# Token lists in tiles of their own, two gathers in flight, and accumulating stores that do not wait for each other, in a fused attention and top-2 mixture-of-experts kernel

## The chip, the cores and the metric

The kernel runs on one core of a Trainium2 chip. The core has five engines that each take their own instructions strictly in order: TensorE (PE), VectorE (DVE), ScalarE (ACT), GpSimd (POOL) and SyncE (SP, which here only issues transfers); 16 DMA engines serve all transfers. The metric is the device time of one execution in microseconds (us): for the kernel before, the median of three runs.

## The reference

Attention over 32 learned memory slots, then a noisy top-2 gate over 8 experts, then the two chosen experts for each of 4608 tokens:

```python
a = softmax(phi, axis=2)                                  # 8 batches x 8 heads x 576 x 32
k_m = einsum('bhsm,bhsd->bhmd', a, k); v_m = einsum('bhsm,bhsd->bhmd', a, v)
x = softmax(q @ k_m.T / 8) @ v_m                          # reshaped to [4608, 512]
z = x @ w_gate + log1p(exp(x @ w_noise)) * noise          # [4608, 8]
top2, top2_w = the two largest of z, and softmax over these two
for e in range(8):
    for k in range(2):
        mask = top2[:, k] == e
        h = relu(x[mask] @ w1[e])                         # 512 -> 1024
        out[mask] += top2_w[mask, k] * (h @ w2[e])        # 1024 -> 512
```

The answer must be close to float32. So every large product is made of float16 halves: a value is split into a high and a low part, and three products (high by high, high by low, low by high) are summed.

## The kernel before, in words

**Attention and routing (to about 277 us).** The tokens are worked on in four pairs of batches of nine 128-token tiles each. The pieces of work of attention, of the routing and of the first expert's early groups are sorted by a table of times written by hand (`PRI`), and a scheduler, which simulates the engines, sets from these priorities the order in which each engine gets its instructions. `gate()` decides for a pair of batches which two experts each token goes to and which slot of that expert's list it takes. It writes one (token row, weight) entry per token and choice into the table `lst` in device memory: a scatter on POOL (L514), one for each tile and each of the two choices, 72 in all. The last pair is gated in two parts, of five tiles (10 scatters) and of four (8 scatters).

**The lists.** Each expert has a list of 1216 slots: nine tiles of 128 tokens and a tail of 64. `lists(e, t0, t1)` reads a piece of it into the tile `lt` (SP, L609). Tiles of that name come from a pool with two buffers: the list of expert e+1 takes the buffer of expert e-1. Each read names all scatters recorded so far as things to wait for; a scatter that comes after a read of `lst` waits for that read.

**Groups.** Experts work on groups of four, four and two list tiles (4 x 128, 4 x 128, 128 + 64 tokens). Expert 0 has four groups, and its first three, of two tiles, start before the routing is complete; so does the fetching for expert 1's first group, whose four tiles surely hold only tokens of earlier pairs. For each tile of a group:

- `gather()` fetches the tile's token rows by an indirect DMA on POOL (`gtile`, L652, 80 in all), splits them into float16 halves on ACT (`ghalf`, L665) and DVE (L666), and puts the transposed halves into `xt` by a transposing DMA on SP (L667). `gtile` and `ghalf` have two buffers each, `xt` three.
- `mm1()` makes the hidden layer in eight blocks of 128 features: 12 matmuls into a PSUM tile `mp` (L702, three buffers), a relu on ACT (`r`, L706) and the split on DVE (`hh`, L707; `hl`, L708).
- `mm2()` makes the output of each 128-token tile from 24 matmuls (L734; `ps`, three buffers); ACT scales it by the token weights (`y`, L738, two buffers). The tail of 64 goes through L744, L748, L749 and L750.
- `put()` adds `y` to the rows of `out` that the list names: an accumulating indirect DMA on POOL (L759, 74 from `y` and 6 early ones from `stg`). All of them write the same tensor, so each waits until the one before has landed.

**The order in the experts' phase.** The loop over (expert, group) starts the gathers two groups ahead of the matmuls and steps through them between pieces of `mm1` and `mm2`. At the first group of expert e it also issues the loads of expert e+1's weights (`stg`, L550, SP: two matrices of four 512 KB pieces), and reads expert e+1's list. The weights are split on ACT (`wh`, L584) and DVE (`wl`, L585) after a maximum over each piece (`wam`, L567). SP's queue thus holds list reads, weight loads and transposes in one row, POOL's queue gathers and stores. What of these stands first in a queue holds up all that stands behind it until its own wait ends. The last tile of expert e-1 is stored after the matmuls of that expert's last group, and the list of expert e+1, for which it frees the buffer, is read behind it.

Of the kernel before, what the change touches and what calls it, by code (L numbers as in the profile page):

```python
# [20 lines left out]
NP = B // 2  # L21
# [18 lines left out]
F32G = 0  # L40
HC = 2.0 ** -14
# [4 lines left out]
def tile_attn_moe(ctx, tc, q_t, phi_t, kv, wgn, noise, w1, w2, out, dbg=None):  # L46
# [56 lines left out]
    # row h*32+m of a group keeps its own head's columns  # L103
# [14 lines left out]
    def late_consts():  # L118
        scr = ld.tile([128, 2, S], F32, name="qs", bufs=BUF["qs"])
        scr = scr.rearrange("p a s -> p (a s)")  # L120
        pidx = scr[:, 0:128].bitcast(I32)
        G.iota(pidx, pattern=[[1, 128]], base=0, channel_multiplier=-1)
        V.tensor_scalar(tri, pidx, 0.0, None, op0=OP.is_gt)
        G.iota(iota_e, pattern=[[0, NJ], [1, E]], base=0, channel_multiplier=0,
               allow_small_or_imprecise_dtypes=True)
        G.iota(eoff, pattern=[[0, NJ], [LCAP, E]], base=0, channel_multiplier=0,
               allow_small_or_imprecise_dtypes=True)
        V.memset(base, 0.0)
        G.memset(zt, 0.0)
        # token lists start as trash rows with weight zero  # L130
        pl = scr[:, 424:424 + 2 * NPRE].rearrange("p (c t) -> p c t", t=2)
        pi = scr[:, 128:128 + NPRE].bitcast(I32)
        G.iota(pi, pattern=[[1, NPRE]], base=0, channel_multiplier=NPRE)
        V.tensor_scalar(pi, pi, TRASH - 1, None, op0=OP.bitwise_and)
        G.memset(pl, 0.0)
        V.tensor_copy(pl[:, :, 0].bitcast(I32), pi)
        nc.sync.dma_start(lst.rearrange("(p c) t -> p (c t)", p=128), pl.rearrange("p c t -> p (c t)"))
        nc.sync.dma_start(xs[0:TRASH, :].rearrange("(a p) d -> p a d", p=128), zt[:, None, :].to_broadcast([128, TRASH // 128, DM]))
# [12 lines left out]
    def overflow_count():  # L151
        # 128-token blocks of each expert beyond its static slots, and the sums of their counts
# [26 lines left out]
    def overflow():  # L179
        # tokens of an expert beyond its static slots, 128 at a time  # L180
# [116 lines left out]
    def a_s(u):  # L297
        """Scores, memory slots on the partitions; a batch's 64 tokens beside the next one's in tile 4."""
        b, g = divmod(u, 2)
        if g == 0:  # L300
            ST[b] = wk.tile([128, 2, 640 - b % 2 * 128], F32, name="st%d" % (b % 2), bufs=BUF["st%d" % (b % 2)])
        for o, n in ((0, 512), (512, 64)) if b % 2 == 0 else ((0, 64), (64, 512)):
            sp = px.tile([128, 512], F32, name="xp")
            for hp in range(2):
                T.matmul(sp[hp * 64:(hp + 1) * 64, 0:n], KB[u][:, hp * 64:(hp + 1) * 64],
                         QS[u][:, hp, o:o + n], start=True, stop=True)
            dst = ST[b][:, g, o:o + n] if b % 2 == 0 else ST[b][:, g, 0:512] if o else ST[b - 1][:, g, 576:640]
            A.activation(dst, sp[:, 0:n], AF.Copy)
# [11 lines left out]
    def scale_chain(pool, psp, am, n, tag):  # L320
        # a power of two that brings the largest magnitude below 2^10
# [102 lines left out]
    scatters, gated = [], set()  # L424

    def gate(P, j0, j1):
# [15 lines left out]
        # log1p(exp(z)) = ln(1+u) u / ((1+u)-1), and u where 1+u == 1  # L442
# [32 lines left out]
        # slot of a token in its experts' lists: earlier pairs, earlier tiles, earlier rows  # L475
# [36 lines left out]
        for j in range(nj):  # L512
            for k in range(2):
# [3 lines left out]
                for o in scatters:  # L517
                    tc.declare_no_dep(sc.ins, o.ins, reason="distinct list slots")
                scatters.append(sc)
# [5 lines left out]
    late = {}  # L525
    W, WS, WU, LT, XT, HT = {}, {}, {}, {}, {}, {}

    def rows(t):
        return 128 if t < NTL else TAIL
# [7 lines left out]
    def w_load(e, i):  # L537
        if e == 0 and F32G:
            # expert 0's early groups multiply in float32, while the other engines are busy
# [18 lines left out]
    def w_prep(e, i):  # L558
        """Split one of the expert's matrices, scaled by a power of two, into high and low parts."""
# [42 lines left out]
    def lists(e, t0, t1):  # L602
        if e not in LT:
            LT[e] = msm.tile([128, NTL + 1, 2], F32, name="lt")
# [3 lines left out]
        def read(dst, src):  # L608
            d = nc.sync.dma_start(dst, src)  # L609
            for s in scatters:  # L610
                tc.add_manual_dep(d.ins, s.ins.name, SYNC, reason="list entries")
# [25 lines left out]
    def gather(e, g):  # L637
# [10 lines left out]
        XT[e, g] = xt  # L648
        for i, t in enumerate(ts):
            n = rows(t)  # L650
            gt = mpool.tile([128, DM], F32, name="gtile", bufs=2)
            G.indirect_dma_start(  # L652
                out=gt[:n], out_offset=None, in_=xs[0:seen, :],
                in_offset=bass.IndirectOffsetOnAxis(ap=LT[e][:n, t, 0:1].bitcast(I32), axis=0))
            yield
            if e == 0 and g < F32G:
                ps = mps.tile([128, 512], F32, name="mp")
                for c in range(4):
                    T.transpose(ps[:, c * 128:c * 128 + n], gt[:n, c * 128:(c + 1) * 128], identf[:n, :n])
                A.activation(xt[:, :, i * 128:i * 128 + n],  # L660
                             ps.rearrange("p (c n) -> p c n", c=4)[:, :, 0:n], AF.Copy)
                yield
                continue
            gh = mpool.tile([128, 2, DM], F16, name="ghalf", bufs=2)
            A.activation(gh[:n, 0], gt[:n], AF.Copy)  # L665
            V.tensor_tensor(gh[:n, 1], gt[:n], gh[:n, 0], OP.subtract)  # L666
# [3 lines left out]
    def hbuf(e, g):  # L670
        if e == 0 and g < 3:
            # the eight row blocks of the hidden layer, float32
# [81 lines left out]
    def put(e, t, y):  # L754
# [7 lines left out]
        if e == E - 1:  # L762
            # of two neighbouring tiles, unused slots have trash rows of their own
            if (t, NTL) == (NTL - 1, late.get("last")):
                tc.declare_no_dep(d.ins, late["lastd"].ins, reason="distinct rows")
            late["last"], late["lastd"] = t, d
# [24 lines left out]
    def unit(u):  # L791
        # the first units have no work beside them: their stages follow one another at once
# [38 lines left out]
    def early(e, g, t, t1, md):  # L831
        """Work of expert e's token group g before the routing is complete."""
# [80 lines left out]
    if dbg is not None:  # L913
        nc.sync.dma_start(dbg["xs"], xs[TRASH:, :])
        nc.sync.dma_start(dbg["lst"], lst)
        nc.sync.dma_start(dbg["cnt"], base)
# [10 lines left out]
    wt(1, 4, NTL + 1)  # L927
    seq = [(0, 3), (1, 1), (1, 2)] + [(e, g) for e in range(2, E) for g in range(3)]
# [4 lines left out]
    for k, (e, g) in enumerate(seq):  # L933
        if e and g == (1 if e == 1 else 0):
            if e + 1 < E:
# [3 lines left out]
                lists(e + 1, 0, NTL + 1)  # L939
# [59 lines left out]
```

## Time and profile before

| | |
|---|---|
| time, three runs | 1083.1, 1087.76, 1075.59 us (median 1083.1) |
| the profiled execution | 1082.0 us, its span 1082.0 us |
| PE busy | 965.0 us (89%), 5632 matmuls |
| DVE, ACT, POOL busy | 530.8, 371.5, 331.0 us |
| DMA | 147.93 MB, mean 137 GB/s |
| attention and routing, with early groups of expert 0 | to about 277 us |
| experts | 277 to 1067 us, then the last stores |
| PE idle in the experts' phase, 297 to 1067 us | 39.3 us, in a dozen gaps of up to 9.47 us |

PE is busy for most of the experts' phase, so the gaps between its matmuls are what to look at there: for each the trace names what ended it. "Releaser" means the instruction or transfer that the waiting one waited for last. The granted clock (PEclk) tells where PE ran below full speed; its mean in a window of 1.00 is full speed, and 0.50 would be half throughout.

### The profile page before, as it was taken

The numbers are of one execution on the slowest core, as the hardware profiler recorded it, in microseconds if no ns is written. First come the engines' busy times: TensorE is split into PE (matmuls) and PEld (weight loads), VectorE is DVE, ScalarE is ACT, GpSimd is POOL, SyncE is SP. The second block draws the span as 40 slices with busy tenths as digits, with TensorE's granted clock in tenths as the row PEclk, the third lists the DMA queues.
The fourth block names the chain that finished last, engine by engine and source line by source line (L and its number), as shares of the span: only waits on it lengthen the run. The fifth ranks groups of instructions, "written<-read, shape, count | busy, mean of one in ns | idle before, by whom it ended". The sixth has DMA issues, their size and how long they took to land.

```text
span 1082.0 us, 15210 instructions
## 1 busy us (share of the span) xinstructions
PE 965.0 (89%) x5632; PEld 496.2 (46%) x5632; DVE 530.8 (49%) x1391; ACT 371.5 (34%) x760; POOL 331.0 (31%) x314
## 2 busy tenths in 40 slices
PE   5897888486986978998998999999899999999995
PEld 3464555254433434543553454446344544454453
DVE  3689787574242523874273338744523573323212
ACT  4676562332122312532232234333222543221211
POOL 2133637654432123223213131322231143211111
PEclk9899889689998989999999999999999999999998
DMA  9999999767374365665445256645453436430212
GB/s 313 336 364 353 226 340 270 166 131 114 69 171 74 98 93 112 142 164 133 84 117 118 39 91 187 178 88 77 124 115 67 87 78 125 74 54 8 37 24 31
DMA packets 144874, 147.93 MB, mean 137 GB/s; under 512 B 94176, under 2 KB 103456, under 8 KB 144800
## 3 DMA queue, kind: packets, MB, share of 16 engines
q1 hardware_dynamic: 125344, 107.02, 36.5%
q0 software_dynamic: 19456, 39.93, 21.6%
q8 instruction: 45, 0.74, 0.3%
q14 instruction: 29, 0.24, 0.1%
HBM read 86.77 MB, written 40.22 MB: 117 GB/s over the span
## 4 chain that ended last, share of the span: by engine, by line
PE 46%; DMA 15%; DVE 6%; issue 3%; POOL 1%; ACT 1%; POOLq 0%; ACTq 0%; SPq 0%; DVEq 0%
PE ps L734 25%; PE mp L702 20%; DMA gtile<-xs,lt 7%; DMA out<-y,lt 5%; DVE wl L585 3%; DMA xt<-ghalf 2%; DMA stg<-in_w 1%; DVE wam L567 1%; PE ps L744 1%; DMA lt<-lst 1%; POOL gtile L652 1%; POOL out L759 1%; DVE hh L707 0%; ACT ghalf L665 0%; DVE hl L708 0%
## 5 line engine op out<-in xcount | busy, mean ns | idle before, releaser
L702 PE MATMUL mp<-xt,wh 128*128 128x512 f16 (+2 forms) x1408 | 283.8, 339 | 22.5 <-ACT r L706 13.0
L759 POOL DMA_INDIRECT out<-y,lt x74 | 117.5, 1588 | 367.8 <-ACT y L738 164.2
L702 PEld LDWEIGHTS <-wh 128*128 128x128 f16 x1600 | 152.2, 99 | 154.9 <-issue 40.1
L734 PE MATMUL ps<-wh,hh 128*128 128x512 f16 x496 | 186.6, 384 | 12.1 <-DVE hh L707 6.1
L707 DVE CAST hh<-r 128x512 f16<-128x512 f32 (+3 forms) x200 | 72.6, 365 | 241.7 <-ACT r L706 240.9
L734 PE MATMUL ps<-wh,hl 128*128 128x512 f16 x496 | 189.8, 384 | 0.7 <-DVE hl L708 0.6
L734 PE MATMUL ps<-wl,hh 128*128 128x512 f16 x496 | 189.3, 383 | 0.0
L734 PEld LDWEIGHTS <-hh 128*128 128x128 f16 x1152 | 114.0, 99 | 144.8 <-issue 10.8
L706 ACT ACTIVATE r<-mp 128x512 f32<-128x512 f32 (+3 forms) x200 | 96.9, 492 | 228.9 <-PE mp L702 161.8
L652 POOL DMA_INDIRECT gtile<-xs,lt x80 | 89.5, 1118 | 228.8 <-DVE ghalf L666 154.0
L702 PE MATMUL mp<-xt,wl 128*128 128x512 f16 (+2 forms) x704 | 153.0, 340 | 0.0
L666 DVE TENSOR_TENSOR ghalf<-gtile,ghalf 128x512 f16<-128x512 f32 x80 | 55.1, 690 | 155.6 <-ACT ghalf L665 155.6
L708 DVE TENSOR_TENSOR hl<-r,hh 128x512 f16<-128x512 f32 (+3 forms) x200 | 113.4, 570 | 4.8
L665 ACT ACTIVATE ghalf<-gtile 128x512 f16<-128x512 f32 x80 | 50.2, 628 | 188.9 <-DMA gtile<-xs,lt 138.0
L702 PEld LDWEIGHTS <-wl 128*128 128x128 f16 x800 | 76.8, 99 | 59.6 <-issue 3.3
L567 DVE TENSOR_REDUCE wam<-stg 128x1 f32<-128x512 f32 x128 | 81.7, 678 | 34.2 <-DMA stg<-in_w 34.1
L734 PEld LDWEIGHTS <-hl 128*128 128x128 f16 x576 | 57.2, 99 | 86.7 <-issue 18.3
L738 ACT ACTIVATE y<-ps,wlu 128x512 f32<-128x512 f32 x62 | 42.1, 683 | 154.6 <-PE ps L734 121.6
L514 POOL DMA_INDIRECT lst<-gent,gidx x72 | 72.3, 1004 | 23.5 <-issue 19.0
L585 DVE SCALAR_TENSOR_TENSOR wl<-stg,wsc,wh 128x512 f16<-128x512 f32 x96 | 65.3, 742 | 0.0
L584 ACT ACTIVATE wh<-stg,wsc 128x512 f16<-128x512 f32 x96 | 60.1, 709 | 4.2 <-DVE wsc L332 4.1
L414 PE MATMUL xp<-vb,at 128*128 128x272 f32 (+1 forms) x160 | 48.1, 443 | 14.3 <-ACT xr L416 14.3
(167 smaller groups left out, 819.0 us busy)
## 6 DMA issues: line engine op xcount, KB each, us to landing
stg<-in_w SPq DMA_DIRECT2D x64, 512.0 KB, 7.0
kvs<-in_kv SPq DMA_DIRECT2D x16, 1024.0 KB, 10.3
out<-zt SPq DMA_DIRECT2D x38, 256.0 KB, 5.1
qs<-in_q_t SPq DMA_DIRECT2D x16, 576.0 KB, 10.0
xs<-xr SPq DMA_DIRECT2D x36, 256.0 KB, 6.4
phs<-in_phi_t SPq DMA_DIRECT2D x16, 288.0 KB, 8.7
kvs<-in_kv SPq DMA_DIRECT2D x16, 128.0 KB, 9.8
gtile<-xs,lt POOLq DMA_INDIRECT x80, 4.2
```

Of the source, the lines that this page charges most:

```text
L514: sc = G.indirect_dma_start(out=lst[:, :], out_offset=bass.IndirectOffsetOnAxis(ap=idx[:, j, k:k + 1], axis=0), in_=ent[:, j, k, :], in_of ...
L567: V.tensor_reduce(am[:, c:c + 1], ss[c], axis=AX.X, op=OP.max, apply_absolute_value=True)
L584: A.activation(wh[:, cs], ss[c], AF.Identity, scale=sc)
L585: V.scalar_tensor_tensor(wl[:, cs], ss[c], sc, wh[:, cs], op0=OP.mult, op1=OP.subtract)
L652: G.indirect_dma_start(out=gt[:n], out_offset=None, in_=xs[0:seen, :], in_offset=bass.IndirectOffsetOnAxis(ap=LT[e][:n, t, 0:1].bitcast(I3 ...
L666: V.tensor_tensor(gh[:n, 1], gt[:n], gh[:n, 0], OP.subtract)
L702: T.matmul(ps[:, :n], ww[:, c * FF + f * 128:c * FF + (f + 1) * 128], xt[:, xo + c, :n], start=(k == 0), stop=(k == 11))
L706: A.activation(r[:, :n], ps[:, :n], AF.Relu, scale=HC)
L707: V.tensor_copy(hh[:, f, :n], r[:, :n])
L708: V.tensor_tensor(hl[:, f, :n], r[:, :n], hh[:, f, :n], OP.subtract)
L734: T.matmul(ps, hs[:, i * 128:(i + 1) * 128], ws, start=(k == 0), stop=(k == 8 * m - 1))
L759: d = G.indirect_dma_start(out=out[:, :], out_offset=bass.IndirectOffsetOnAxis(ap=LT[e][:n, t, 0:1].bitcast(I32), axis=0), in_=y[:n], in_o ...
```

## The change

1. `lt` gets eight buffers, one for each expert. The lists of experts 2 to 7 are all read in one go, right behind those of experts 0 and 1, ahead of the loop over the experts.
2. A list read names only the scatters whose slots it can hold: an early read for expert 0's group g those of pairs 0 to g, the read for expert 1's first four tiles those of the first three pairs, all others all. Reads and later pairs' scatters are declared independent of one another.
3. `gtile` gets three buffers, and `gather()` issues the fetch of tile i+1 before it splits tile i.
4. The stores of one expert are declared independent of one another: an expert names a row at most once, and unused slots have trash rows of their own. A store of the next expert still waits for those of the one before. The special case that the last expert had for two of its tiles is dropped.

```diff
+GT = 3
@@ gate() @@
-                for o in scatters:
+                for _, o in scatters:
                     tc.declare_no_dep(sc.ins, o.ins, reason="distinct list slots")
-                scatters.append(sc)
+                scatters.append((P, sc))
+                for p, o in reads:
+                    if p < P:
+                        tc.declare_no_dep(sc.ins, o.ins, reason="slots of earlier pairs")
@@ lists() @@
-            LT[e] = msm.tile([128, NTL + 1, 2], F32, name="lt")
+            LT[e] = msm.tile([128, NTL + 1, 2], F32, name="lt", bufs=E)
...
-            for s in scatters:
-                tc.add_manual_dep(d.ins, s.ins.name, SYNC, reason="list entries")
+            last = t1 // 2 - 1 if e == 0 and t1 <= 6 else NP - 2 if (e, t1) == (1, 4) else NP - 1
+            for p, s in scatters:
+                if p <= last:
+                    tc.add_manual_dep(d.ins, s.ins.name, SYNC, reason="list entries")
+                else:
+                    tc.declare_no_dep(d.ins, s.ins, reason="slots of earlier pairs")
+            reads.append((last, d))
@@ gather() @@
+        gts = {}
+        def fetch(i):
+            t = ts[i]
+            n = rows(t)
+            gts[i] = mpool.tile([128, DM], F32, name="gtile", bufs=GT)
+            G.indirect_dma_start(
+                out=gts[i][:n], out_offset=None, in_=xs[0:seen, :],
+                in_offset=bass.IndirectOffsetOnAxis(ap=LT[e][:n, t, 0:1].bitcast(I32), axis=0))
         for i, t in enumerate(ts):
             n = rows(t)
-            gt = mpool.tile([128, DM], F32, name="gtile", bufs=2)
-            G.indirect_dma_start(
...
-            yield
+            for k in range(i if i == 0 else i + 1, min(i + 2, len(ts))):
+                fetch(k)
+                yield
...
-            A.activation(gh[:n, 0], gt[:n], AF.Copy)
-            V.tensor_tensor(gh[:n, 1], gt[:n], gh[:n, 0], OP.subtract)
+            A.activation(gh[:n, 0], gts[i][:n], AF.Copy)
+            V.tensor_tensor(gh[:n, 1], gts[i][:n], gh[:n, 0], OP.subtract)
@@ put() @@
-        if e == E - 1:
...
-            late["last"], late["lastd"] = t, d
+        for o in PUT.setdefault(e, []):
+            tc.declare_no_dep(d.ins, o.ins, reason="distinct rows")
+        PUT[e].append(d)
@@ the experts' phase @@
     lists(1, 4, NTL + 1)
     wt(1, 4, NTL + 1)
+    for e in range(2, E):
+        lists(e, 0, NTL + 1)
...
                 w_load(e + 1, 1)
-                lists(e + 1, 0, NTL + 1)
```

Every engine gets the same instructions as before, in another order and with other waits. Because lines were added, the line numbers of the changed kernel differ: scatter L515, gather L664, `ghalf` L675 and L676, `r` L716, `y` L748, store L769, list read L613, weight load L554, transpose L677.

**First place: POOL while the last pair is gated.** `lst<-gent,gidx` is a scatter, `gtile<-xs,lt` a gather (first two of expert 0's third group, then four of expert 1's first), `out<-stg,lt` an early store. Before:

```order
L495 IOTA gent 128x10
L652 DMA gtile<-xs,lt 128x512 x2
L514 DMA lst<-gent,gidx 37888x2 x10
L652 DMA gtile<-xs,lt 128x512 x2
L495 IOTA gent 128x8
L759 DMA out<-stg,lt 4864x512
L652 DMA gtile<-xs,lt 128x512
L759 DMA out<-stg,lt 4864x512
L652 DMA gtile<-xs,lt 128x512
L759 DMA out<-stg,lt 4864x512
L514 DMA lst<-gent,gidx 37888x2 x8
```

The changed kernel, the same stretch:

```order
L496 IOTA gent 128x10
L515 DMA lst<-gent,gidx 37888x2 x6
L664 DMA gtile<-xs,lt 128x512 x2
L515 DMA lst<-gent,gidx 37888x2
L664 DMA gtile<-xs,lt 128x512
L515 DMA lst<-gent,gidx 37888x2 x3
L664 DMA gtile<-xs,lt 128x512 x3
L769 DMA out<-stg,lt 4864x512
L496 IOTA gent 128x8
L769 DMA out<-stg,lt 4864x512 x2
L515 DMA lst<-gent,gidx 37888x2 x8
```

Six scatters that stood behind the first two gathers now stand ahead of them; the gathers for expert 1 have moved up among the scatters and ahead of the early stores.

**Second place: POOL in a middle expert, with what each instruction waits for.** DMASW is a transfer that POOL issued, DMAHW one of SP's, Activation and DVE are those engines. Before, the end of one expert and the start of the next list's gathers:

```order
L759 DMA out<-y,lt 4864x512 [waits DMASW5_49,Activation_49]
L759 DMA out<-y,lt 4864x512 [waits DMASW0_49,Activation_49]
L759 DMA out<-y,lt 4864x512 [waits DMASW1_49,Activation_49]
L759 DMA out<-y,lt 4864x512 [waits DMASW2_49,Activation_49]
L759 DMA out<-y,lt 4864x512 [waits DMASW3_49,Activation_49]
L759 DMA out<-y,lt 4864x512 [waits DMASW4_49,DVE_49]
L652 DMA gtile<-xs,lt 128x512 [waits DMAHW2_49,DMASW6_49]
L652 DMA gtile<-xs,lt 128x512 [waits DMASW7_49]
L652 DMA gtile<-xs,lt 128x512 [waits DMASW6_49,DVE_49]
```

The changed kernel, from the first store of an expert on:

```order
L769 DMA out<-y,lt 4864x512 [waits DMASW3_49,DMASW2_49,DMASW6_49,DMASW1_49,Activation_49]
L769 DMA out<-y,lt 4864x512 [waits Activation_49]
L664 DMA gtile<-xs,lt 128x512 [waits DMASW5_49,DVE_49]
L664 DMA gtile<-xs,lt 128x512 [waits DMASW7_49,DVE_49]
L769 DMA out<-y,lt 4864x512 [waits Activation_49] x2
L664 DMA gtile<-xs,lt 64x512 [waits DMAHW3_49,DMASW0_49,DVE_49]
L664 DMA gtile<-xs,lt 128x512 [waits DMAHW4_49,DMASW3_49,DVE_49]
L769 DMA out<-y,lt 4864x512 [waits DMASW1_49,Activation_49]
L664 DMA gtile<-xs,lt 128x512 [waits DMASW4_49,DMASW2_49,DVE_49]
L664 DMA gtile<-xs,lt 128x512 [waits DMASW7_49,DVE_49]
```

Only an expert's first store names several earlier stores; the gathers of the next expert have moved up among the stores, where before they stood behind the last of them.

**Third place: ACT in the first two groups of an expert.** `r` is the relu of one block of `mm1`, `y` the scaling of one tile of `mm2`, `ghalf` the first half of a tile of a later group. Before:

```order
L706 ACTIVATE r<-mp 128x512 x4
L665 ACTIVATE ghalf<-gtile 128x512 x2
L706 ACTIVATE r<-mp 128x512 x4
L665 ACTIVATE ghalf<-gtile 128x512 x2
L738 ACTIVATE y<-ps_5777,wlu 128x512
L665 ACTIVATE ghalf<-gtile 128x512 x2
L738 ACTIVATE y<-ps_5808,wlu 128x512
```

The changed kernel, the same group:

```order
L716 ACTIVATE r<-mp 128x512 x8
L675 ACTIVATE ghalf<-gtile 128x512 x3
L748 ACTIVATE y<-ps_5786,wlu 128x512
L675 ACTIVATE ghalf<-gtile 128x512
L748 ACTIVATE y<-ps_5817,wlu 128x512
```

The eight `r` of a group now stand together, and three `ghalf` in a row stand between the last `r` and the first `y`.

More of the change, by code (lines that the diff above doesn't have):

```diff
@@ L45, in tile_attn_moe @@
 @with_exitstack
-def tile_attn_moe(ctx, tc, q_t, phi_t, kv, wgn, noise, w1, w2, out, dbg=None):
+def tile_attn_moe(ctx, tc, q_t, phi_t, kv, wgn, noise, w1, w2, out):
     nc = tc.nc
@@ L421, in c_av @@
         V.tensor_tensor(LG[P][:, j], xr[:, 0, 256:], xr[:, 1, 256:], OP.add)
-    scatters, gated = [], set()
+    scatters, reads, gated = [], [], set()
     def gate(P, j0, j1):
@@ L525, in tile_attn_moe @@
     late = {}
-    W, WS, WU, LT, XT, HT = {}, {}, {}, {}, {}, {}
+    W, WS, WU, LT, XT, HT, PUT = {}, {}, {}, {}, {}, {}, {}
     def rows(t):
@@ L648, in gather @@
         XT[e, g] = xt
+        gts = {}
[6 more added lines that the diff above has]
+                in_offset=bass.IndirectOffsetOnAxis(ap=LT[e][:n, t, 0:1].bitcast(I32), axis=0))
         for i, t in enumerate(ts):
             n = rows(t)
-            gt = mpool.tile([128, DM], F32, name="gtile", bufs=2)
-            G.indirect_dma_start(
-                out=gt[:n], out_offset=None, in_=xs[0:seen, :],
-                in_offset=bass.IndirectOffsetOnAxis(ap=LT[e][:n, t, 0:1].bitcast(I32), axis=0))
-            yield
[L656 to L661, printed above, removed]
+            for k in range(i if i == 0 else i + 1, min(i + 2, len(ts))):
+                fetch(k)
                 yield
-                continue
             gh = mpool.tile([128, 2, DM], F16, name="ghalf", bufs=2)
-            A.activation(gh[:n, 0], gt[:n], AF.Copy)
-            V.tensor_tensor(gh[:n, 1], gt[:n], gh[:n, 0], OP.subtract)
+            A.activation(gh[:n, 0], gts[i][:n], AF.Copy)
+            V.tensor_tensor(gh[:n, 1], gts[i][:n], gh[:n, 0], OP.subtract)
             nc.sync.dma_start_transpose(xt[:, :, i * 128:i * 128 + n], gh[:n].rearrange("p a d -> p (a d)"))
@@ L761, in put @@
             in_=y[:n], in_offset=None, compute_op=OP.add)
-        if e == E - 1:
-            if (t, NTL) == (NTL - 1, late.get("last")):
-                tc.declare_no_dep(d.ins, late["lastd"].ins, reason="distinct rows")
-            late["last"], late["lastd"] = t, d
+        for o in PUT.setdefault(e, []):
+            tc.declare_no_dep(d.ins, o.ins, reason="distinct rows")
+        PUT[e].append(d)
     def run(it, n=10 ** 9):
@@ L912, in tile_attn_moe @@
     tc.cur_priority = int(P0 + 60 * 2000)
[L913 to L916, printed above, removed]
     ats.close()
```

## The prediction

> **What bounds the kernel now.** I read the page first, then PE in windows around its gaps, then the chain of waits there. The windows' columns are length, busy time and count of each engine, granted clock (PEclk), DMA share and GB/s.
>
> ```profile
> span 1082.0 us, 15210 instructions
> ...
> core 0: us, PE busy (x) PEld busy (x) DVE busy (x) ACT busy (x) POOL busy (x), PEclk, DMA share, GB/s
> 297.00:343.00 46.00, 32.61 (x141) 14.45 (x139) 17.22 (x31) 11.58 (x20) 14.69 (x12) 0.85 0.68 142
> 380.00:414.00 34.00, 22.57 (x89) 8.83 (x87) 10.46 (x18) 7.09 (x13) 9.10 (x9) 0.85 0.64 106
> 470.00:500.00 30.00, 25.24 (x109) 10.57 (x107) 18.24 (x32) 11.74 (x20) 10.45 (x8) 0.94 0.72 173
> 560.00:582.00 22.00, 19.26 (x83) 8.34 (x82) 11.69 (x22) 4.99 (x9) 5.32 (x5) 0.92 0.35 87
> 690.00:702.00 12.00, 10.08 (x47) 4.40 (x47) 7.58 (x14) 2.41 (x4) 6.35 (x4) 1.00 1.05 285
> 770.00:790.00 20.00, 17.21 (x73) 7.35 (x72) 8.82 (x17) 4.65 (x8) 5.07 (x5) 0.91 0.37 87
> 880.00:902.00 22.00, 19.81 (x85) 8.26 (x83) 12.31 (x22) 9.20 (x16) 11.39 (x6) 0.92 0.45 101
> ```
>
> Length minus PE's busy time is idle: 13.4 us in the first window and 11.4, 4.8, 2.7, 1.9, 2.8 and 2.2 us, together 25.8, in the six that follow. Elsewhere in the experts' phase PE has hardly a gap:
>
> ```profile
> 580.00:650.00 70.00, 70.00 (x379) 35.52 (x377) 22.23 (x48) 20.38 (x35) 18.39 (x14) 1.00 0.49 81
> ```
>
> A gap costs more than itself. The windows that begin where PE resumes show it:
>
> ```profile
> 301.59:307.00 5.41, 5.41 (x18) 2.14 (x18) 5.41 (x11) 2.15 (x4) 1.59 (x2) 0.68 0.41 100
> 335.89:341.00 5.11, 5.11 (x18) 2.21 (x18) 1.56 (x4) 1.51 (x3) 1.59 (x1) 0.65 0.69 103
> 395.10:401.10 6.00, 6.00 (x15) 2.11 (x15) 2.67 (x6) 1.07 (x2) 0.94 (x1) 0.52 1.16 150
> 413.10:419.10 6.00, 5.98 (x20) 2.32 (x21) 2.08 (x3) 1.83 (x3) 1.79 (x2) 0.72 0.72 175
> 491.77:497.77 6.00, 6.00 (x21) 2.38 (x21) 3.36 (x7) 1.44 (x3) 2.95 (x3) 0.72 0.90 191
> 575.43:581.43 6.00, 6.00 (x22) 2.39 (x22) 4.38 (x9) 1.63 (x3) 0.94 (x1) 0.75 0.43 112
> 699.90:705.90 6.00, 5.97 (x28) 2.73 (x28) 3.47 (x7) 1.19 (x2) 2.96 (x3) 1.00 0.99 198
> 781.96:787.96 6.00, 6.00 (x21) 2.34 (x20) 4.45 (x9) 1.63 (x3) 0.94 (x1) 0.72 0.44 119
> 894.50:900.50 6.00, 5.98 (x20) 2.19 (x21) 3.97 (x7) 1.74 (x3) 2.43 (x3) 0.72 0.69 155
> ```
>
> Length times (1 - PEclk) is lost to the clock: 1.7 and 1.8 us behind the first window's two large gaps, and 2.9, 1.7, 1.7, 1.5, 0, 1.7 and 1.7, together 11.1, behind the others. [...]
>
> The chain of waits (start, duration) through one of the six windows, and the wait tables (total, times, longest) of POOL, ACT and SP:
>
> ```profile
> 383.53 3.67 DMA out<-y,lt
> 387.25 1.56 DMA lt<-lst
> ...
> 389.07 1.01 POOL gtile L652
> ```
>
> ```profile
> SPq L609 <- DMA out<-y,lt: 77.4, 10, 13.8
> ...
> POOL out L759 <- DMA out<-y,lt: 104.2, 25, 8.5
> ```
>
> A store must land before SP may read the list into its buffer, the list must land before POOL may gather, and ACT's `ghalf` then stands in front of a relu for which PE waits. The 104.2 us are stores one behind another; gathers queue behind them.
>
> **The change part by part.**
>
> *Lists (-36.9).* The list reads of experts 2 to 7 no longer wait for a store, and stores of one expert no longer for each other (the order shows it: they name ACT alone). Gathers move up among the stores, a group earlier. So the chain above is gone in all six windows: 25.8 idle and 11.1 clock. At most that; at the least nothing, if another wait ends last (rivals). I take all, since the fully busy window shows that ACT, DVE and POOL have time to spare when gathers are early.
>
> *The first window (-8.2 of 16.9).* It holds expert 0's last group and expert 1, whose lists stay behind the last scatters. Its first gathers and its end:
>
> ```profile
> 293.21 8.74 DMA gtile<-xs,lt x2
> ...
> 319.36 5.50 DMA out<-y,lt
> ```
>
> ```profile
> 334.64 0.63 ACT L665 ACTIVATE ghalf<-gtile 128x512 f16<-128x512 f32 x1 [7.48 <-DMA gtile<-xs,lt]
> ```
>
> ```profile
> gtile<-xs,lt POOLq DMA_INDIRECT x80, 4.2
> xt<-ghalf SPq DMA_TRANSPOSE x74, 4.1
> ...
> L665 ACT ACTIVATE ghalf<-gtile 128x512 f16<-128x512 f32 x80 | 50.2, 628 | 188.9 <-DMA gtile<-xs,lt 138.0
> L666 DVE TENSOR_TENSOR ghalf<-gtile,ghalf 128x512 f16<-128x512 f32 x80 | 55.1, 690 | 155.6 <-ACT ghalf L665 155.6
> ```
>
> The first gather cannot start earlier than 293.2; with the usual 4.2 us of landing behind 1.0 of issue, and the weight loads, which ran beside it, now two transposes later in SP's queue, it is there at 298.4. Then the two `ghalf` buffers set the pace: 0.63 on ACT, 0.69 on DVE and 4.1 to the transpose's landing are 5.4 us for two tiles; I add 1.2 for what stands in the queues between, an estimate, which makes 3.3 each. The tenth tile comes at 298.4 + 9 x 3.3 = 328.1 in place of 334.6, since its gather no longer stands behind a store that waits for another's landing (5.50). The gap of 9.5 us there shrinks to some 3, the gap of 3.9 at the window's start to 3, with 1.7 and 1.0 of clock: 8.7 of 16.9 us stay. Bounds: 0 and 16.9 won. [...]
>
> *The last pair (+2).* Six scatters now stand ahead of the first two gathers:
>
> ```profile
> L514 POOL DMA_INDIRECT lst<-gent,gidx x72 | 72.3, 1004 | 23.5 <-issue 19.0
> ...
> 232.79 1.02 POOL L652 DMA_INDIRECT gtile<-xs,lt  x1 [2.85 <-DMA lt<-lst]
> ...
> 225.00:277.00 52.00, 41.04 (x273) 25.50 (x270) 25.89 (x106) 10.76 (x27) 22.05 (x23) 0.97 0.61 120
> ```
>
> Each takes 1.0 and 0.3 of issue, 7.7 together; they fill the 2.85 us for which POOL waited, so the gathers, and the matmuls fed by them, come about 5 us later. PE has 11.0 us of gaps in that window, most behind the gating that follows; expert 1's gathers and its list read come earlier. I take 2 of 5 as not covered. Bounds: -3 (a gap closes) and +7.7 (no cover).
>
> *Twelve list reads ahead of the loop (0).*
>
> ```profile
> 288.69 3.35 SPq L609 DMA_DIRECT2D lt<-lst  x4
> ```
>
> ```profile
> L609 SPq DMA_DIRECT2D lt<-lst x20: 326/423/1707, 135.1 to 879.8; - x20
> ```
>
> Behind the four reads of before, which end at 292.0, they take 12 x 0.42 = 5 us of SP, to 297, ahead of the weight loads and the first transpose, which needs the first `ghalf` at 298.4. Were that cover gone, the 5 us would lie in the first window.
>
> *New order on ACT (+3).* Three `ghalf` now stand between the last relu and the first `y`. The third needs the first tile's transpose: 0.63 + 0.69 + 4.1, and with its own 0.63 and about as much for `y`, the first `y` is done some 6.7 us after the last relu.
>
> ```profile
> 579.63 20.72 PE ps L734 x96
> ```
>
> Four tiles take 20.7 us, so the fourth needs the first tile's PSUM buffer 15.5 us behind the start: covered by nearly 9 us. I leave 0.5 us for each of experts 2 to 7, bounds 0 and R1's 22.
>
> The sum: 1082.0 - 36.9 - 8.2 + 2 + 3 = 1041.9, say **1042 us**. The profiled execution stands 1.1 us under the median of the three runs, 1083.1, which lie within 12 us; I make no correction.
>
> **The rivals.**
>
> *R1: the stores become the late ones.* Stores now stand behind gathers that wait for a `gtile` buffer, so behind a `ghalf` that is late. `y` has two buffers, and ACT waits for a store already now:
>
> ```profile
> ACT y L738 <- DMA out<-y,lt: 33.0, 9, 5.7
> ```
>
> At 33.0 / 9 = 3.7 us once in each of experts 2 to 7, 22 us come back: 1064. Against it: a store's own wait for the store before is gone.
>
> *R2: slower.* Transposes now stand behind whole weight loads in SP's queue, and a load waits for its staging buffer:
>
> ```profile
> SPq L550 <- DVE wsa L326: 71.8, 3, 25.2
> ...
> SPq L550 <- DVE wl L585: 56.2, 8, 23.4
> ```
>
> If `ghalf` buffers stay full behind such a load, ACT stands, then `y`, then PE after its 15.5 us of cover: 25.2 - 15.5 + 1.7 of clock = 11.4 us a time. With all eleven waits of these rows it is +125, 1167 us. It decides from five on (+57: 1099); three or four leave no change. Against it: such waits lay beside fully busy stretches already.
>
> *R3: the waits stay in some other form,* no change, 1082. The order, in which the stores name ACT alone and the gathers stand among them, speaks against it.
>
> **How the numbers follow.** Forecast 0.66 (its own range 1026 to 1056: the floor without any gap or slow clock from 297 us on is 1082.0 - 53.8 = 1028, and the last pair may give 3 more). R1 0.20, within 1056 to 1071. No change within 1% (about what a measurement of this kernel can tell), 0.08: R3 and the mild part of R2. Slower by over 1%, 0.06: R2. Faster 0.86. The range 1026 to 1068 leaves out those 0.14 and a little at either side.
>
> **What would show it.** After: no wait of a list read for a store, hardly any of a store for a store; PE over 99% busy from 345 to 1066 us, at full clock; in the first window 6 to 10 us less idle, with gathers in pairs; from 225 to 277 some 11 to 14 us idle. The prediction is wrong if gaps of 2 us or more stay in every expert: behind `y` (R1) or behind a `ghalf` that waits for a transpose (R2).

## The result, and the profile after

The changed kernel takes 1054.46 us (median of four runs, 1051.79 to 1055.06); the kernel before took 1085.09 us beside it (1075.59 to 1087.76). The ratio is 0.972, with a 95% interval of 0.966 to 0.977: 31 us faster. The forecast was 1042 (1026 to 1068). It was summed from the span of a profiled execution, from its first to its last instruction; the changed kernel's profiled execution spans 1053.0 us, 11 above it. The time of a run is 1.7 to 2.3 us longer than its span in all the runs here that have both.

Four of the windows of before, the first of them to 345 us and not 343, asked of the changed kernel (length, busy time and count of each engine, PEclk, DMA share, GB/s); the last row is the experts' phase from 360 us on:

```profile
297.00:345.00 48.00, 37.71 (x168) 16.66 (x167) 18.38 (x34) 11.29 (x19) 20.00 (x18) 0.96 0.90 178
...
380.00:414.00 34.00, 32.91 (x156) 14.74 (x153) 15.39 (x28) 10.03 (x17) 7.58 (x6) 1.00 0.53 121
470.00:500.00 30.00, 29.68 (x139) 13.37 (x138) 14.54 (x25) 7.15 (x12) 10.55 (x8) 1.00 0.84 153
560.00:582.00 22.00, 22.00 (x103) 9.96 (x102) 4.63 (x8) 4.96 (x8) 8.68 (x7) 1.00 0.64 123
360.00:1037.00 677.00, 675.40 (x3606) 332.08 (x3605) 315.73 (x661) 218.04 (x384) 164.80 (x123) 1.00 0.49 99
```

From 360 us on PE is idle for 1.6 us in all and the clock is full (PEclk 1.00). The gaps that the lists and stores made are gone. The first window has 10.3 us of idle left (13.4 in the same stretch of before).

What the engines wait for now, from 297 us to the last matmul (total, times, longest):

```profile
POOL gtile L664 <- DVE ghalf L676: 265.2, 37, 22.6
...
ACT ghalf L675 <- DMA xt<-ghalf: 133.9, 57, 9.4
...
ACT y L748 <- DMA out<-y,lt: 14.1, 4, 4.0
...
ACT ghalf L675 <- DMA gtile<-xs,lt: 8.4, 2, 7.7
...
PE mp L712 <- ACT y L748: 6.7, 2, 3.7
```

No row has a list read that waits for a store, and none a store that waits for a store. In this part of the executions ACT's waits for gathers fell from 132.2 us to 8.4, and its waits for transposes, which free `ghalf` buffers, rose from 39.6 to 133.9: the next link of the same chain. PE does not feel it, but for the 6.7 us of the last row, which lie in the first window. ACT's waits for `y` buffers (stores) fell from 33.0 to 14.1.

To tell apart where the time went, the table cuts each profiled execution at three matmuls: the first of expert 0's second early group, the first on `xt` (expert 1's first group), and the first of expert 1's second group. The experts' start is the second cut; "window" is from it to the third, and "rest" from there to the last matmul.

| kernel | second early group at | experts' start at | window | rest |
|---|---|---|---|---|
| before | 218.6 | 276.8 | 95.1 | 697.9 |
| changed | 224.6 | 286.4 | 94.0 | 660.6 |
| lists alone | 216.7 | 276.3 | 97.0 | 671.7 |
| stores alone | 226.0 | 288.1 | 87.5 | 674.1 |
| two gathers alone | 225.9 | 289.4 | 88.2 | 694.2 |
| changed, without the early slots | 225.8 | 290.1 | 95.1 | 658.6 |
| changed, lists read late | 228.1 | 291.3 | 96.0 | 661.7 |
| changed, one gather in flight | 226.4 | 290.0 | 85.8 | 660.7 |
| lists and stores | 225.9 | 288.4 | 91.0 | 659.4 |
| changed, only expert 1's slots early | 223.8 | 289.1 | 93.6 | 658.7 |
| changed, counting first | 222.5 | 287.5 | 87.9 | 658.6 |
| before, counting first | 224.9 | 285.9 | 92.0 | 691.1 |
| one gather, three `ghalf`, counting first | 224.3 | 284.6 | 86.4 | 658.6 |
| lists late, counting first | 224.9 | 286.6 | 90.2 | 658.7 |

Before to changed: +9.6 to the experts' start, -1.1 in the window, -37.3 in the rest, -0.2 in the last stores: -29.0, which is 1053.0 - 1082.0.

### The profile page after: what moved, and what is told of

It reads as the page before. It is cut to its first block, busy times and chain, and to the rows that moved or that the text cites. A ratio compares the mean times of both kernels' runs of the same rounds, so it can differ in the third digit from the quotient of the medians.

```text
span 1053.0 us, 15157 instructions
## 1 busy us (share of the span) xinstructions
PE 954.6 (91%) x5632; PEld 495.4 (47%) x5632; DVE 527.7 (50%) x1391; ACT 372.0 (35%) x760; POOL 324.1 (31%) x314
## 3 DMA queue, kind: packets, MB, share of 16 engines
q1 hardware_dynamic: 125344, 107.02, 37.3%
## 4 chain that ended last, share of the span: by engine, by line
PE 53%; DMA 7%; DVE 6%; issue 4%; POOL 1%; ACT 1%; SPq 1%; POOLq 0%; ACTq 0%; DVEq 0%
PE mp L712 26%; PE ps L744 25%; DVE wl L589 3%; DMA xt<-ghalf 3%; DMA stg<-in_w 2%; DVE wam L571 1%; PE ps L754 1%; DMA out<-y,lt 1%; POOL out L769 1%; DVE ghalf L676 1%; DVE hl L718 1%; SPq L677 1%; DMA gtile<-xs,lt 0%; DVE hh L717 0%; POOL lst L515 0%
## 5 line engine op out<-in xcount | busy, mean ns | idle before, releaser
L769 POOL DMA_INDIRECT out<-y,lt x74 | 117.9, 1593 | 274.3 <-ACT y L748 246.6
L716 ACT ACTIVATE r<-mp 128x512 f32<-128x512 f32 (+3 forms) x200 | 97.5, 493 | 265.0 <-PE mp L712 180.8
L744 PE MATMUL ps<-wh,hh 128*128 128x512 f16 x496 | 183.8, 379 | 0.0
L664 POOL DMA_INDIRECT gtile<-xs,lt x80 | 81.8, 1022 | 289.4 <-DVE ghalf L676 265.2
L676 DVE TENSOR_TENSOR ghalf<-gtile,ghalf 128x512 f16<-128x512 f32 x80 | 54.5, 688 | 117.6 <-ACT ghalf L675 110.6
L712 PEld LDWEIGHTS <-wl 128*128 128x128 f16 x800 | 77.4, 100 | 60.9 <-issue 3.0
L675 ACT ACTIVATE ghalf<-gtile 128x512 f16<-128x512 f32 x80 | 49.8, 628 | 157.8 <-DMA xt<-ghalf 138.1
L748 ACT ACTIVATE y<-ps,wlu 128x512 f32<-128x512 f32 x62 | 41.9, 680 | 131.6 <-PE ps L744 113.8
L515 POOL DMA_INDIRECT lst<-gent,gidx x72 | 72.8, 1011 | 30.4 <-issue 19.7
```

The lines of the kernel that those rows point to most:

```text
L515: sc = G.indirect_dma_start(out=lst[:, :], out_offset=bass.IndirectOffsetOnAxis(ap=idx[:, j, k:k + 1], axis=0), in_=ent[:, j, k, :], in_of ...
L664: G.indirect_dma_start(out=gts[i][:n], out_offset=None, in_=xs[0:seen, :], in_offset=bass.IndirectOffsetOnAxis(ap=LT[e][:n, t, 0:1].bitcas ...
L676: V.tensor_tensor(gh[:n, 1], gts[i][:n], gh[:n, 0], OP.subtract)
L712: T.matmul(ps[:, :n], ww[:, c * FF + f * 128:c * FF + (f + 1) * 128], xt[:, xo + c, :n], start=(k == 0), stop=(k == 11))
L716: A.activation(r[:, :n], ps[:, :n], AF.Relu, scale=HC)
L744: T.matmul(ps, hs[:, i * 128:(i + 1) * 128], ws, start=(k == 0), stop=(k == 8 * m - 1))
```

## The experiments

### Lists, stores and gathers, each alone

**Lists alone,** on the kernel before.

```diff
-            LT[e] = msm.tile([128, NTL + 1, 2], F32, name="lt")
+            LT[e] = msm.tile([128, NTL + 1, 2], F32, name="lt", bufs=E)
...
+    for e in range(2, E):
+        lists(e, 0, NTL + 1)
...
-                lists(e + 1, 0, NTL + 1)
```

> The kernel before, with list tiles of their own and all lists read ahead of the loop; stores still wait for each other, one gather in flight. Theory (the list read behind the last store is the wait that ends last in the six later windows): PE's gaps after 345 us fall from 25.8 to under 5 us and the time by 28 to 36 us, to about 1050. Rival (the stores' landings hold the gathers, the list only repeats that wait): the gaps after 345 us stay over 15 us and the time falls by under 15 us, to about 1070.

1063.58 us, ratio 0.981 (0.971 to 0.991). PE's idle time after 345 us:

```profile
345.00:1040.00 695.00, 686.86 (x3641) 336.75 (x3639) 320.45 (x670) 220.83 (x387) 168.36 (x125) 0.99 0.48 97
```

8.1 us remain, nearly all of it two gaps of 3.9 in which PE waits for a relu. The rest of the experts' phase is 26.2 us shorter, seven tenths of what the whole change took from it. Neither the gaps nor the time fits the theory or the rival. The chain behind the first of the two gaps:

```profile
476.79 0.70 DVE ghalf L666
477.50 0.26 issue
477.76 0.33 POOL gtile L652
478.08 0.95 issue
479.04 5.24 DMA out<-y,lt
...
484.38 0.69 ACT y L738
485.07 0.49 ACT r L706
485.57 0.04 issue
485.61 0.59 PE mp L702
```

A gather that waited for a late `ghalf` holds the store behind it on POOL's queue, the store holds a `y` buffer, and `y` the relu. That is the mechanism of the prediction's R1; in this kernel it came in two of the six later experts, and cost PE 3.9 us each time.

**Stores alone,** on the kernel before.

```diff
-        if e == E - 1:
...
-            late["last"], late["lastd"] = t, d
+        for o in PUT.setdefault(e, []):
+            tc.declare_no_dep(d.ins, o.ins, reason="distinct rows")
+        PUT[e].append(d)
```

> The kernel before, with the stores of one expert independent of each other; lists read one expert at a time into two buffers. Theory: the list still waits for the last store of the expert before, which lands once and not behind five others, so the gaps after 345 us shrink by a third at most: 8 to 12 us faster, about 1073. Rival (the stores are the cause): 25 us or more faster, about 1055.

1059.93 us, ratio 0.972 (0.963 to 0.981): 28 us. That is the rival's size, and my theory of a third at most falls. The waits of the two kernels, lists alone and then stores alone, show why both help and neither suffices (the second has its rows of POOL and of SP apart):

```profile
POOL out L759 <- DMA out<-y,lt: 69.2, 18, 4.5
```

```profile
POOL gtile L652 <- DMA lt<-lst: 47.5, 7, 10.2
```

```profile
SPq L609 <- DMA out<-y,lt: 60.3, 10, 13.9
```

With lists alone, stores still wait for stores; with stores alone, SP's list read still waits for a store (60.3 us, 77.4 before) and the gathers for the list. But the last store of an expert no longer has a row of others to wait for, so the list is late by less: the first list read of the loop comes 5.8 us behind the third cut of the table, where before it came 15.4 behind. The rest is 23.8 us shorter. The window is 7.6 us shorter too, and that is not clearly the stores' doing: the scheduler put part of the routing's work earlier in this kernel (the section on one gather tells why that matters).

**Both,** on the kernel before: the two edits together.

```diff
+            LT[e] = msm.tile([128, NTL + 1, 2], F32, name="lt", bufs=E)
...
+        for o in PUT.setdefault(e, []):
+            tc.declare_no_dep(d.ins, o.ins, reason="distinct rows")
```

> The kernel before with its own list tiles, all lists read ahead of the loop, and independent stores; one gather in flight, and all list reads tied to all scatters. Theory (lists and stores together are the whole of the gain, each alone leaves the other's wait): the same as the changed kernel within 3 us, 1051 to 1057, no gap over 1 us after 360 us. Rival (either alone is all of it): as with the stores alone, gaps of some 10 us after 360 us stay, about 1060.

1054.11 us, ratio 0.967 (0.958 to 0.976); the rest is 38.5 us shorter and has 0.5 us of gaps. 26.2 and 23.8 alone, 38.5 together: they share 11.5, which fits two links of one chain. The theory holds, and with these two edits the kernel is within 1 us of the changed one. Its window, 3.0 us shorter than the changed kernel's, has the same earlier routing as with the stores alone.

**Two gathers alone,** on the kernel before.

```diff
-            gt = mpool.tile([128, DM], F32, name="gtile", bufs=2)
+            gts[i] = mpool.tile([128, DM], F32, name="gtile", bufs=GT)
...
+            for k in range(i if i == 0 else i + 1, min(i + 2, len(ts))):
+                fetch(k)
```

> The kernel before, with three gather buffers and each fetch issued one tile ahead; lists and stores as before. Theory: the six later windows stay as they are (lists and stores hold the gathers), only the window from 297 to 343 us gains a little: 0 to 5 us faster, 1079 to 1084. Rival (gathers one after another set the pace of each group): 10 us or more faster, under 1074.

1085.32 us, ratio 0.996 (0.991 to 1.000). The rest is 3.7 us shorter and keeps 26.1 us of gaps, as the theory has it; the window is shorter by 6.9.

### The scatters ahead of the gathers

The changed kernel without its second part:

```diff
-                for p, o in reads:
-                    if p < P:
-                        tc.declare_no_dep(sc.ins, o.ins, reason="slots of earlier pairs")
...
-                if p <= last:
-                    tc.add_manual_dep(d.ins, s.ins.name, SYNC, reason="list entries")
-                else:
-                    tc.declare_no_dep(d.ins, s.ins, reason="slots of earlier pairs")
+                tc.add_manual_dep(d.ins, s.ins.name, SYNC, reason="list entries")
```

> The changed kernel without its second part: every list read waits for all scatters recorded so far, and later scatters wait for it, as before; so the first gathers stand ahead of the last pair's first ten scatters again. Theory (these scatters ahead of the gathers delay the early groups, and cost some 5 us of what is missing against the forecast): 3 to 7 us faster than the changed kernel, about 1049. Rival (the delay is covered, the missing time lies in chance or elsewhere): the same as the changed kernel within 2 us, about 1054; or slower by up to 5, if the earlier gathers for expert 1 were worth something.

1057.53 us, ratio 0.972 (0.964 to 0.981): no faster than the changed kernel, as the rival has it. From the second early group to the experts' start it takes 290.1 - 225.8 = 64.3 us, against 61.9 in the changed kernel.

The changed kernel, with only the read of expert 1's first slots free of later scatters:

```diff
-            reads.append((last, d))
+            if e == 1:
+                reads.append((last, d))
```

> The changed kernel, but later scatters wait for expert 0's early list reads again; only the read of expert 1's first slots is free of them, so the gathers of expert 0's third group stand ahead of the scatters as before, and only expert 1's first gather is drawn among them. Theory (six scatters ahead of two gathers cost 3 to 4 us between the first matmul of expert 0's second early group and that of expert 1's, where the changed kernel took 61.8 us and the kernel before 58.2): 57 to 60 us there. Rival (the cost there comes from the order on ACT, where three ghalf stand ahead of the scaling of the second group's output, which stays): 61 to 65 us.

1058.15 us, ratio 0.972 (0.963 to 0.982); 65.3 us in that stretch: the theory falls, and the number lies just above the rival's 61 to 65. So the six scatters ahead of two gathers cost nothing that shows. The kernels with the order of before in that stretch (stores alone, two gathers alone) take 62.1 and 63.5. Only the profiled executions of before and of lists alone, which reach the second early group 6 to 8 us earlier than the changed one, take 58.2 and 59.6. What the rival says of ACT's order was not tried by itself.

### The twelve list reads

The changed kernel, with the reads back in the loop, each placed on SP's queue behind the latest transpose, without a wait:

```diff
-    for e in range(2, E):
-        lists(e, 0, NTL + 1)
...
                 w_load(e + 1, 1)
+                lists(e + 1, 0, NTL + 1)
...
             d = nc.sync.dma_start(dst, src)
+            if e > 1:
+                tc.add_manual_dep(d.ins, late["tp"].ins.name, ORDER, reason="order")
...
```

> The changed kernel, but each list of experts 2 to 7 is read in the loop again, into its own tile, ordered on SP's queue behind a transpose that is already recorded, so that SP has no twelve reads in a row ahead of the first transposes. Theory (the twelve reads, which took 10.1 us of SP together with the four before them, hold the transposes and with them the ghalf buffers in the first window): from the first matmul on expert 1's tokens to the last matmul it takes 3 to 8 us less than the changed kernel's 754.6, 747 to 752, with the first window's gaps at 6 us or less. Rival (the window is bound by gathers and transposes landing one after another, the reads are hidden): 753 to 757, gaps of 12 us as before.

1060.45 us, ratio 0.971 (0.962 to 0.979); window 96.0, from the experts' start to the last matmul 757.7. The rival holds, within 1 us: the reads, though long, hold nobody up that PE waits for. SP in the changed kernel (start, duration):

```profile
298.92 10.14 SPq L613 DMA_DIRECT2D lt<-lst  x16
309.17 2.62 SPq L677 DMA_TRANSPOSE xt<-ghalf  x2
```

The late reads once more, with the routing's counting matmuls early too (their edit stands below):

```diff
+                tc.add_manual_dep(d.ins, late["tp"].ins.name, ORDER, reason="order")
...
+        t = add_low(t + PRI["g2"], -9.0 if j0 else 0, run, g, 1)
```

> The kernel with late list reads and the counting matmuls first, otherwise as changed. Theory (the twelve reads ahead of the loop cost nothing): the same as with the counting matmuls alone, within 2 us, from the first matmul on expert 1's tokens to the last. Rival (once the gathers are early, SP's 10 us of list reads are the next wait): 3 to 6 us less than that.

1051.0 us, ratio 0.970 (0.961 to 0.979); 748.9 us from the experts' start, against 746.5 with the counting alone. The rival falls; the theory's 2 us are missed by 0.4, on the side of more time.

### One gather in flight, and what it turned up

The changed kernel, with one gather in flight:

```diff
-GT = 3
+GT = 2
...
-            for k in range(i if i == 0 else i + 1, min(i + 2, len(ts))):
-                fetch(k)
-                yield
+            fetch(i)
+            yield
```

> The changed kernel with two gather buffers and one gather in flight, as before. Theory (two in flight only serve the first window, where the ghalf buffers set the pace anyway): within 3 us of the changed kernel, 1052 to 1058; from the first matmul on expert 1's tokens to the last 753 to 758. Rival (two in flight are a real part of the gain): 8 us or more slower, over 1062.

1051.79 us, ratio 0.966 (0.958 to 0.973): if anything faster than the changed kernel, and 746.5 us from the experts' start in place of 754.6. The rival falls, and the theory's 753 to 758 us are missed too. The difference lies in the window, and POOL tells where it begins: the last eight scatters start 19.2 us ahead of the experts' start in this kernel, and 0.3 us ahead in the changed one and in the kernel before. In the changed kernel the DVE operation that ends the last choice of experts, the matmuls that count the tokens from it, and the first scatter (start, duration):

```profile
263.46 0.18 DVE L474 TENSOR_TENSOR gmb<-gk,gk 128x32 bf16<-128x32 f32 x1
```

```profile
283.76 0.24 PE L485 MATMUL tr<-gmb,ones_bf 128*128 128x8 bf16 x4
```

```profile
286.18 1.00 POOL L515 DMA_INDIRECT lst<-gent,gidx  x1 [1.64 <-DVE onit L171]
```

Four matmuls of 0.24 us together wait 20 us in PE's queue behind those of expert 0's third group, although what they read is there. On them hang the slots, the scatters, the last lists and the first gathers of the phase. With one gather in flight the scheduler happened to put them first. The next kernel is the changed one with the priority of this one step of the gating raised, for the last part of the last pair (in `routing()`). The step holds eight counting matmuls, of which these four and one more had come late, and the slot arithmetic behind them:

```diff
-        t = add(t + PRI["g2"], run, g, 1)
+        t = add_low(t + PRI["g2"], -9.0 if j0 else 0, run, g, 1)
```

> The changed kernel; only the priority of the last pair's counting matmuls (eight tiny ones) is raised, so that they stand ahead of the 96 matmuls of expert 0's third group and not behind most of its second product. Theory (the late start of the last eight scatters is what kept the first window's gain away: they began 0.3 us ahead of the first matmul on expert 1's tokens, and 19.2 us ahead with one gather in flight, where the counting came early by chance of the order): scatters 12 us or more ahead, gaps in the first window under 8 us (13.2), from that first matmul to the last 744 to 749 us (754.6). Rival (two gathers in flight are what costs the window, the scatters do not matter): 752 to 757 us, gaps over 11.

1048.9 us, ratio 0.968 (0.959 to 0.978). The scatters start 18.6 us ahead of the experts' start, 746.5 us follow it, and the window's gaps are 6.4 us.

```profile
264.94 0.18 PE L480 MATMUL tr<-gmb,tri 128*128 128x32 bf16 x1
264.96 0.22 PE L482 MATMUL tr<-gmb,ones_bf 128*128 128x24 bf16 x3
265.04 0.24 PE L485 MATMUL tr<-gmb,ones_bf 128*128 128x8 bf16 x4
```

```profile
268.89 1.04 POOL L515 DMA_INDIRECT lst<-gent,gidx  x1 [1.88 <-DVE hh L717]
...
278.44 0.97 POOL L515 DMA_INDIRECT lst<-gent,gidx  x1 [0.30 <-issue]
285.66 0.99 POOL L664 DMA_INDIRECT gtile<-xs,lt  x1 [6.26 <-DMA lt<-lst]
```

The theory holds in all its numbers. The first gather of the phase stands 1.8 us ahead of the experts' start; in the changed kernel it came 16.4 us after it.

The medians of the two kernels are 5.6 us apart, and their intervals overlap; the 8.1 us (754.6 - 746.5) compare one execution of each. But four variants of the changed kernel have the counting early, and take 745.0 to 748.9 us from the experts' start; the changed kernel and three more have it late, and take 752.3 to 757.7. With one gather in flight (and the counting early by the scheduler's choice) and with two it is the same 746.5 us: the second gather in flight is worth nothing that shows here.

The scheduler's choice bears on two earlier results as well: with the stores alone, and with lists and stores, the last eight scatters start 6.2 us ahead of the experts' start, where before and lists alone have 0.3. So some of what their windows gained may be the counting's; that was not tried by itself.

**The same edit on the kernel before.**

```diff
-        t = add(t + PRI["g2"], run, g, 1)
+        t = add_low(t + PRI["g2"], -9.0 if j0 else 0, run, g, 1)
```

> The kernel before, with the same raised priority and nothing else. Theory (the late counting is a loss of its own, independent of lists and stores): from the first matmul on expert 1's tokens to the last 782 to 788 us (793.0), gaps after the first window unchanged at some 26 us, time 5 to 10 us less than before. Rival (stores that wait for each other hold the gathers in the first window anyway): 791 to 795 us.

1081.13 us, ratio 0.993 (0.989 to 0.998): 6 us, with 783.1 us from the experts' start (793.0) and 24.2 us of gaps after the window. The late counting is a loss of its own, which the change neither made nor removed.

**Three `ghalf` buffers,** with one gather in flight and the counting first.

```diff
-            gh = mpool.tile([128, 2, DM], F16, name="ghalf", bufs=2)
+            gh = mpool.tile([128, 2, DM], F16, name="ghalf", bufs=3)
```

> The changed kernel with two gather buffers and one gather in flight, but three ghalf buffers in place of two, and the counting matmuls first. Theory (transposes that hold the two ghalf buffers set the pace in the first window, and ACT's waits for transposes show it): 742 to 745 us from the first matmul on expert 1's tokens to the last (746.5 with two buffers), gaps under 4 us there (6.0), time about 1048. Rival (the window is by now bound by the start of the gathers alone): 746 to 748 us.

1046.94 us (1043.52 to 1051.95), ratio 0.965 (0.956 to 0.974). The waits did what was meant; counting first with two `ghalf` buffers, then this kernel:

```profile
ACT ghalf L675 <- DMA xt<-ghalf: 123.8, 55, 9.3
```

```profile
ACT ghalf L674 <- DMA xt<-ghalf: 37.3, 26, 2.6
...
ACT ghalf L674 <- DMA gtile<-xs,lt: 80.6, 29, 8.0
```

But from the experts' start it takes 745.0 us, 1.5 less than without, and 7.4 us of gaps stay in the window. That is inconclusive for PE: the wait moved back to the gathers. It has the lowest median here; its interval overlaps those of counting first and of the changed kernel.

## Why the prediction was right, and where its terms were off

**Lists: right.** Forecast -36.9 us; with the new order on ACT (+3) it is one stretch, the rest of the experts' phase, which became 37.3 us shorter. Both parts of the sum are there: PE's idle time in the rest fell from 25.9 to 1.6 us (forecast 25.8 won), and the clock came back with the gaps. PEclk is 1.00 from 360 us on; in before the rest, with a mean PEclk of 0.98 over its 697.9 us, held 27.3 us at half clock, which lose 13.7 (forecast 11.1: the slow stretch behind the longest gap lasted 10.2 us, from 390.67 us on, and was counted over 6). The step "at the least nothing, if another wait ends last" did not come true. What I told wrongly on the way is the weight of the two links, which the forecast took together: the stores alone are worth about as much as the lists.

**ACT's new order: nothing, not +3.** PE has 1.6 us of idle after 360 us with three `ghalf` ahead of the first `y`. The wait was covered, as the nearly 9 us in the forecast would have it.

**The first window: -1.1 us, not -8.2.** This is the term that was mis-sized by its mechanism. I wrote that the first gather "cannot start earlier than 293.2". It could: 293.2 was 16.4 us behind the experts' start, and the changed kernel's first gather came at 302.84, again 16.4 behind it. Within the window I counted gathers and `ghalf` buffers and did not ask why the scatters ahead of them ran so late; the counting matmuls, ready 20 us before, were the answer, and putting them first gave 8.1 us. The part of this term that rested on two gathers in flight came to nothing: 746.5 us from the experts' start with one and with two. The estimate of 3.3 us for a tile was low: from the first `ghalf` to the tenth the changed kernel takes 32.2 us, 3.6 each, where before took 34.2; the transposes on the chain through the window took 4.7 to 7.7 us, where I put 4.1. And the last `y` stands behind two more, of expert 2's first group:

```profile
345.54 0.63 ACT L675 ACTIVATE ghalf<-gtile 128x512 f16<-128x512 f32 x1 [3.00 <-DMA xt<-ghalf]
346.08 0.67 ACT L748 ACTIVATE y<-mp,wlu 128x512 f32<-128x512 f32 x1
```

The same edit of two gathers made the window 6.9 us shorter on the kernel before, with the counting just as late, and nothing when it came with the rest. There the last two `y` stand together in ACT's order, here each behind `ghalf`s of its own. That this is the cause is argued, not shown.

**The last pair: +9.6 us, not +2.** But 6.0 of it lie ahead of 224.6 us, where no engine's order differs, and the remaining 3.6 do not go away when the order is undone (two experiments). Of 14 profiled executions, 12 reach the second early group at 222.5 to 228.1 us, stores alone and two gathers alone on the kernel before among them; before and lists alone do so at 218.6 and 216.7. So the profiled execution that I summed from was a short one in this part, and the term for the scatters is 0 within what these runs tell. As a whole it was short by less: its span of 1082.0 us makes a time of some 1084, by the 1.7 to 2.3 us between span and time, against medians of the kernel before of 1085 to 1088 us in four series. (The prediction set the span beside the times as it stood, 1.1 us under their median.) The medians give 31 us for the change, the experts' phase of the two profiled executions 38.4 (37.3 + 1.1). Runs of one kernel lie up to 16 us apart and one execution of each is profiled, so how much of these 7 us is chance, and how much a cost ahead of the experts, stays open.

**The rivals.** R1, late stores: ACT's waits for stores fell, from 33.0 to 14.1 us. Its mechanism was no fancy, though: with the lists alone it made the two gaps of 3.9 us. R2, transposes behind weight loads: ACT's waits for transposes did rise, from 44.6 to 138.1 us in all; PE lost 6.7 us behind them in the first window, and hardly anything after it. R3: the waits are gone.

**The twelve list reads** were forecast at 0 with 5 us on SP; they took over 7 of the 10.14 us that all sixteen took, and cost nothing that shows.

## What to carry to other kernels

Where a buffer's reuse, a chain of writes to one tensor and an in-order queue stand in one line, removing one of them pays only in part, and the gains overlap: 26 and 24 us alone, 38 together here. A gap's releaser is the last link, so follow the chain to the start of what it waits for: a few tiny matmuls in the wrong place of PE's queue were worth 8 us of the profiled execution, and no list of costly groups names them. Sum against more than one profile where you can, since one execution may be 6 us short in a stretch that the change never touches.

## What the runs showed of the hardware

Executions differ in one stretch of the attention phase. From 165 to 190 us, before and then the changed kernel, whose instructions stand in the same order there:

```profile
165.00:190.00 25.00, 20.99 (x144) 13.42 (x142) 16.89 (x55) 6.28 (x19) 18.96 (x19) 0.99 1.04 262
```

```profile
165.00:190.00 25.00, 16.48 (x90) 9.92 (x88) 10.96 (x36) 3.49 (x11) 19.21 (x20) 0.73 0.97 264
```

The changed kernel's waits there, between 165 and 192 us:

```profile
ACT r L716 <- issue: 12.8, 2, 6.9
DVE hh L717 <- issue: 8.3, 2, 4.2
PEld L744 <- issue: 6.6, 12, 2.7
PEld L712 <- issue: 5.7, 10, 0.9
```

Several engines stand without a releaser that the profile shows, with the DMA engines at a share of 0.97 (1.04 before), and the clock falls to 0.73 (0.99 before). The execution with the stores alone has some of it: in the same stretch PE is busy for 18.45 us, at a PEclk of 0.85. What it is was not tried and stays open.

A gap's length alone does not tell whether the clock falls behind it. In the changed kernel, behind gaps of 2.62, 2.73, 3.68 and 3.07 us:

```profile
307.36:313.36 6.00, 6.00 (x28) 2.73 (x28) 4.32 (x9) 2.34 (x4) 2.08 (x2) 1.00 0.87 169
318.45:324.45 6.00, 6.00 (x28) 2.75 (x29) 4.81 (x8) 0.63 (x1) 0.83 (x1) 1.00 1.13 276
339.68:345.68 6.00, 4.05 (x12) 1.56 (x12) 0.79 (x2) 0.77 (x2) 4.47 (x4) 0.72 0.98 193
346.80:352.80 6.00, 6.00 (x23) 2.74 (x23) 3.06 (x7) 1.36 (x3) 2.61 (x2) 0.72 0.61 124
```

The first two kept full speed (PEclk 1.00), the other two did not (0.72); in the kernel before, PEclk was 0.72 to 0.75 over the 6 us behind each of the gaps of 2.19, 2.74 and 2.79 us, and 1.00 behind the one of 1.80. What decides was not shown.
